# A spectral mixer and token MLP on one core: forward FFT over the sequence first, filter loaded in two copies, norm and first product streamed row block by row block

## The chip, the cores and the metric

One NeuronCore of a Trainium2 chip, one launch. The metric is the device time of one execution in microseconds (us). Each comparison ran both kernels on the same chip. A ratio is the mean time of one kernel's runs over the mean of the other's runs in the same rounds, so it is not quite the ratio of the medians quoted beside it. "Span" is the time from the first to the last instruction of the profiled execution; the time of a run is about 1.8 to 2.1 us longer.

Engines: PE is TensorE, DVE is VectorE, ACT is ScalarE, POOL is GpSimd, SP is SyncE, which only issues DMAs here.

## The reference, cut to what matters

```python
x = A_x                                    # [1, 2048, 512] bf16
h  = x + irfft2(rfft2(layernorm(x)) * (A_w_r + 1j * A_w_i))     # over sequence and features
u  = layernorm(layernorm(h))               # both over the 512 features
u  = gelu(einsum("bsd,sf->bdf", u, B_w1) + B_b1)                # 2048 -> 1376 over the sequence
y  = einsum("bdf,fs->bds", u, B_w2) + B_b2                      # 1376 -> 2048
return h + y.transpose(0, 2, 1)
```

## The kernel before

The sequence of 2048 lies in SBUF as 128 partitions by 16 row blocks. The program does not write instructions directly: it declares operations with the tiles they read and write, derives dependencies from the tiles' addresses, lets a list scheduler fix the order on each engine, and turns the remaining dependencies into semaphore waits. Both kernels do this, with two different builders.

```python
def sb_cells(self, ap):                      # which 32-byte cells does this access touch?
    h, lo, hi = self.tensors_by_hname[name]
    offs = np.array([int(ap.offset)], dtype=np.int64)
    dims = list(ap.ap)[1:]                   # the free dimensions; the partition dimension is left out
    for step, n in dims:
        offs = (offs[:, None] + step * np.arange(n)[None, :]).reshape(-1)
    byte_offs = lo + offs * esz
    ...
# op(): a read depends on the cell's last writer; a write on its last writer and all its readers
```

The head of its computation:

```python
for g in range(4):                                           # X in four loads of 512 KB
    dma(f"ld_x{g}", X[:, 4*g:4*g+4, :], x_psd[:, 4*g:4*g+4, :], ...)
dma("ld_wr", Wn[:, 0, :, :], A_w_r.rearrange("(k2 k1) k -> k1 k2 k", k1=NP), ...)   # filter, once
dma("ld_wi", Wn[:, 1, :, :], A_w_i.rearrange("(k2 k1) k -> k1 k2 k", k1=NP), ...)
lw1 = ln_stats(1, lambda s2: X[:, s2, :], NS2, gsz=4, prio=9)                    # DVE
# ... 64 PE transposes of X, then feature DFT: 64 matmuls of 512 columns,
#     rstd applied at the PSUM eviction
# ... 64 transposes of the filter, sequence FFT in two steps with 64 transposes between,
#     24 DVE operations for the complex filter product, inverse FFT,
# ... last inverse product: per row block 4 matmuls of 512 columns + 1 identity matmul adding X
# ... the two norms of h over all 16 blocks, then:
for t in range(NFT):            # first MLP product: 11 tiles x 16 blocks, then GELU in five operations
    for s2 in range(NS2): eng.matmul(ps[0:Mt, bank, :], lhsT, HH[:, s2, :], ...)
for s2 in range(NS2):           # second MLP product: 16 blocks x 11 tiles, bias and residual, store
    ...
```

## Time and profile before

Median 169.18 us of 4 runs (169.15 to 169.22). Span of the profiled run 167.1 us.

| Stretch of the chain | ends at, us |
|---|---|
| X, statistics, transposes, feature DFT | 27.9 |
| filter transposes | 31.4 |
| forward sequence FFT | 45.1 |
| filter product (VectorE) | 59.7 |
| inverse FFT | 67.7 |
| last inverse product | 79.6 |
| norms | 90.4 |
| first MLP product | 125.2 |
| GELU of the last tile | 128.4 |
| second MLP product | 163.7 |
| last block and store | 167.1 |

From the chain of work that ended last, in order of time. Columns: start, duration, engine, tile, line.

```profile
1.13 4.98 DMA X<-in_A_x_dram
6.13 2.48 DVE st_87 L657 x4
...
19.92 7.94 PE ps L738 x36
27.86 3.57 PE ps L719 x64
31.43 7.00 PE ps L769 x64
...
90.42 34.72 PE ps L1009 x160
...
128.35 35.26 PE ps L1033 x162
```

PE's issue intervals can be read here: 34.72 / 160 is 217 ns for 512 columns, 7.00 / 64 is 109 ns for 256, 3.57 / 64 is 56 ns for 128.

### The profile page before, as it was taken

What the parts mean: (1) busy time and instruction counts of PE and PEld (TensorE: products, weight loads), DVE (VectorE), ACT (ScalarE), POOL (GpSimd) and SP (SyncE); (2) the same over time, 40 slices, a digit from 0 to 9 for tenths busy, and PEclk for the clock granted to TensorE, in tenths of its full rate; (3) what the DMA queues carried; (4) which work ended last, traced back from release to release, by engine and by line L of the source; (5) the groups of instructions that cost most, each with busy time, mean ns of one, the idle gap of its engine ahead of it and who ended that gap; (6) DMA issues with size and microseconds to landing.
All of it is one profiled execution on the core that took longest, in us unless ns stands there. A gap on an engine that the chain in (4) does not pass through costs nothing.

```text
span 167.1 us, 2513 instructions
## 1 busy us (share of the span) xinstructions
PE 150.8 (90%) x912; PEld 90.8 (54%) x912; DVE 103.6 (62%) x251; ACT 75.8 (45%) x130; POOL 10.9 (6%) x23
## 2 busy tenths in 40 slices
PE   0599899998998689999995999999999999999991
PEld 0593346987546568544431444444455666666660
DVE  0599981987999979779998454354445322332231
ACT  3075897662599668456885644433432000000000
POOL 0000022200001070200060000000000000000000
PEclk9999999999999999999999999999999999999999
DMA  4999914283006659996039300000000111011101
GB/s 98 372 355 299 404 46 127 45 322 141 4 2 229 277 184 411 389 367 219 4 99 399 129 2 0 0 4 0 0 0 0 63 67 63 33 61 63 63 33 61
DMA packets 10123, 22.71 MB, mean 136 GB/s; under 512 B 928, under 2 KB 7328, under 8 KB 9472
## 3 DMA queue, kind: packets, MB, share of 16 engines
q0 software_dynamic: 2384, 13.90, 22.5%
q1 hardware_dynamic: 7728, 8.66, 15.9%
q8 instruction: 7, 0.11, 0.3%
q14 instruction: 4, 0.03, 0.1%
HBM read 20.46 MB, written 2.10 MB: 135 GB/s over the span
## 4 chain that ended last, share of the span: by engine, by line
PE 67%; DVE 24%; DMA 3%; ACT 3%; issue 1%; SPq 0%; ACTq 0%; DVEq 0%
PE ps L1033 21%; PE ps L1009 21%; DVE st_87 L657 6%; PE ps L918 6%; PE ps L738 5%; PE ps L769 4%; PE ps L892 4%; DMA X<-in_A_x_dram 3%; PE ps L797 2%; DVE st_89 L952 2%; PE ps L719 2%; DVE V_64 L846 1%; DVE V_64 L845 1%; PE ps L910 1%; PE ps L864 1%
## 5 line engine op out<-in xcount | busy, mean ns | idle before, releaser
L1038 DVE SCALAR_TENSOR_TENSOR OUT<-ps,B2f,H 128x512 bf16<-128x512 f32 x16 | 12.0, 751 | 24.2 <-PE ps L1033 24.2
L1009 PE MATMUL ps<-HH,W_b 128*128 128x512 bf16 (+1 forms) x66 | 16.6, 379 | 1.7 <-DVE HH L984 1.5
L918 PE MATMUL ps<-GD,V_51 128*128 128x512 bf16 x64 | 16.4, 379 | 0.0
L1009 PE MATMUL ps<-HH,W_a 128*128 128x512 bf16 (+1 forms) x66 | 16.1, 379 | 0.0
L738 PE MATMUL ps<-Esb,XT 128*128 128x512 bf16 x64 | 14.6, 380 | 1.0 <-DVE D_56 L747 0.6
L657 DVE BATCH_NORM_STATS2 st_87<-X 128x6 f32<-128x512 bf16 x16 | 9.9, 680 | 6.1 <-DMA X<-in_A_x_dram 6.1
L1009 PEld LDWEIGHTS ps<-HH,W_b 128*128 128x128 bf16 (+1 forms) x66 | 6.4, 100 | 10.0 <-DVE HH L984 2.2
L696 PE MATMUL ps<-ID,X 128*128 128x128 bf16 x64 | 6.1, 287 | 6.2 <-DMA X<-in_A_x_dram 6.2
L952 DVE BATCH_NORM_STATS2 st_89<-H 128x6 f32<-128x512 bf16 x16 | 10.8, 686 | 1.3 <-ACT H L926 1.0
L1009 PE MATMUL ps<-HH,W_c 128*128 128x512 bf16 (+1 forms) x44 | 11.3, 379 | 0.0
L738 PEld LDWEIGHTS ps<-Esb,XT 128*128 128x128 bf16 x64 | 5.8, 98 | 9.4 <-ACT XT L703 2.1
L1009 PEld LDWEIGHTS ps<-HH,W_a 128*128 128x128 bf16 (+1 forms) x66 | 6.5, 100 | 7.7 <-ACT HH L983 0.4
L926 ACT ACTIVATE H<-ps 128x512 bf16<-128x512 f32 x13 | 7.7, 595 | 6.4 <-PE ps L918 6.4
L864 PE MATMUL ps<-Hm,V_64 128*128 128x256 bf16 x64 | 8.2, 273 | 2.8 <-ACT TT L877 1.2
L918 PEld LDWEIGHTS ps<-GD,V_51 128*128 128x128 bf16 x64 | 6.2, 98 | 7.5
L830 ACT ACTIVATE Csb<-ps 128x512 bf16<-128x512 f32 x16 | 7.9, 680 | 4.3 <-PE ps L823 4.3
L877 ACT ACTIVATE TT<-ps 128x512 bf16<-128x512 f32 x16 | 8.5, 655 | 2.9 <-PE ps L864 2.8
L696 PEld LDWEIGHTS ps<-ID,X 128*128 128x128 bf16 x64 | 6.0, 134 | 6.2 <-issue 6.2
L864 PEld LDWEIGHTS ps<-Hm,V_64 128*128 128x128 bf16 x64 | 6.0, 98 | 5.0 <-ACT TT L877 2.1
L746 ACT ACTIVATE D_56<-ps,lnw_88 128x512 bf16<-128x512 f32 x13 | 8.1, 694 | 0.6 <-PE ps L738 0.4
L900 DVE CAST V_51<-ps 128x256 bf16<-128x256 f32 x19 | 7.2, 420 | 1.3 <-PE ps L892 1.2
L703 ACT ACTIVATE XT<-ps 128x1024 bf16<-128x1024 bf16 x8 | 7.6, 1017 | 0.0
(118 smaller groups left out, 274.5 us busy)
## 6 DMA issues: line engine op xcount, KB each, us to landing
W_a<-in_B_w_dram POOLq DMA_DIRECT2D x1, 2064.0 KB, 7.6
W_b<-in_B_w_dram POOLq DMA_DIRECT2D x1, 2064.0 KB, 10.4
X<-in_A_x_dram SPq DMA_DIRECT2D x4, 512.0 KB, 6.2
IFP<-c_IFP POOLq DMA_DIRECT2D x1, 2048.0 KB, 9.1
out_dram<-OUT SPq DMA_DIRECT2D x16, 128.0 KB, 1.7
FP<-c_FP SPq DMA_DIRECT2D x1, 1536.0 KB, 10.9
W_c<-in_B_w_dram POOLq DMA_DIRECT2D x1, 1376.0 KB, 6.1
Wn<-in_A_w_r_dram SPq DMA_DIRECT2D x1, 1028.0 KB, 11.0
```

What stands on the lines that cost most here:

```text
L657: o = K.op(f"ln{which}_stats{s2}", "dve", (lambda s, eng, bank, src=src, s2=s2: eng.bn_stats(st[:, s2, 0:6], src)), ins=[src], outs=[st[:, ...
L696: (lambda s, eng, bank, lhsT=lhsT, i=i: eng.matmul(psb[:, bank, i * 128:(i + 1) * 128], lhsT, ID[:, :], is_transpose=True, start=True, sto ...
L738: (lambda s, eng, bank, lhsT=lhsT, rhs=rhs, t=t: eng.matmul(ps[:, bank, :], lhsT, rhs, start=(t == 0), stop=(t == 3))),
L746: return eng.activation(dst, src, ACT.Copy, scale=sc)
L830: return eng.activation(dst, src, ACT.Copy)
L864: eng.matmul(ps[:, bank + ci // 2, (ci % 2) * 256:(ci % 2) * 256 + 256], lhsT, rhs, start=(comp == 0), stop=(comp == 1))),
L877: return eng.activation(dst, src, ACT.Copy)
L918: (lambda s, eng, bank, lhsT=lhsT, rhs=rhs, mi=mi: eng.matmul(ps[:, bank, :], lhsT, rhs, start=False, stop=(mi == 3))),
L952: K.op(f"ln2_stats{s2}", "dve", (lambda s, eng, bank, src=src, s2=s2: eng.bn_stats(st2[:, s2, 0:6], src)), ins=[src], outs=[st2[:, s2, 0:6 ...
L1009: (lambda s, eng, bank, lhsT=lhsT, rhs=rhs, s2=s2, Mt=Mt: eng.matmul(ps[0:Mt, bank, :], lhsT, rhs, start=(s2 == 0), stop=(s2 == NS2 - 1))),
L1033: (lambda s, eng, bank, lhsT=lhsT, rhs=rhs, t=t: eng.matmul(ps[:, bank, :], lhsT, rhs, start=(t == 0), stop=(t == NFT - 1))),
L1038: (lambda s, eng, bank, dst=dst, bia=bia, hs=hs: eng.scalar_tensor_tensor(dst, ps[:, bank, :], bia, hs, op0=ALU.add, op1=ALU.add)),
```

## The change

The intent is to stream fewer columns through PE and to close its holes. The sequence FFT comes first, taken on X itself, so X needs no transposes. The mean is never subtracted: the filter's column for feature frequency 0 is dropped by both kernels. The row scale 1/std is multiplied into the 128 x 128 DFT block of each row block instead of into the data. Real and imaginary parts of a frequency sit on neighbouring partitions, so the filter product is one DVE operation per chunk, and this needs the filter in SBUF twice, once for the real and once for the imaginary row. The inverse is done block by block, and its result goes through residual, norm and six of the eleven tiles of the first MLP product at once. GELU is one ScalarE activation.

The new builder's tracker, the new filter load and the new head, cut to the core (`+` lines of the diff):

```diff
+    def cells_of(self, ap):
+        lo = self.tensors[ap.tensor.name]
+        ...
+        offs = np.array([int(ap.offset)], dtype=np.int64)
+        for step, n in list(ap.ap)[1:]:
+            if n > 1:
+                offs = (offs[:, None] + step * np.arange(n, dtype=np.int64)[None, :]).reshape(-1)
+        b = lo + offs * esz
...
+    pieces = [(0, 8), (8, 18), (18, 32)]
+    for pi, (ta, tb) in enumerate(pieces):
+        for comp, wsrc in enumerate((A_w_r, A_w_i)):
+            q = "sp" if comp == 0 else "pool"
+            for reim in range(2):
+                for j in range(2):
+                    for sgn in range(2):
+                        p0 = 4 * j + 2 * sgn + reim
+                        ...
+                            dma(f"ld_w{comp}_{pi}_{p0}_{a}", q, W[p0:NP:8, a:b, comp, :], src, ...,
+                                prio=1.0 + pi, group=f"W{pi}{q}", wgroup=f"W{pi}")
+    K.op("mk_eps", "dve", lambda e, eng: eng.memset(eps[:, 0:1], LN_EPS), outs=[eps[:, 0:1]], ...)
...
+    for g in range(8):
+        # bn_stats, bn_aggr on DVE; sqrt on ACT ("sd"); reciprocal on DVE ("rs"); then for both blocks
+                K.op(f"fs{n2}_{s}", ("pool" if g < 7 else "dve"),          # scale the DFT block
+                     lambda e, eng, ...: eng.tensor_scalar(FS[:, n2, ...], F[:, n2, :], rs[:, n2, 0:1], ...))
+        # first product: 4 matmuls of 256 columns per block
+        K.op(f"Ye{g}", "act", emit_y, ins=[ps[:, b0:b0 + 2, :]], outs=[dst], ...)
```

## The prediction

> **What bounds the kernel now.** The page gives PE 90% of a 167.1 us span (wall time 169.18, so 2.1 us lie outside it). The chain of waits, in order of time: X lands at 6.1; norm statistics, X transposes and the first product until 27.9; filter transposes to 31.4; forward FFT to 45; the filter multiply, bound by VectorE (24 operations of 0.60 us), to 59.7; inverse FFT to 67.7; last inverse product (64 matmuls plus 16 identity matmuls of 512 columns) to 79.6; a second norm with almost no PE work until 90.4; first MLP product 34.7 us; a GELU chain of 3.2 us; second product 35.3 us; 2.7 us of tail. Full-rate issue intervals from the same chain: 217 ns at 512 columns, 109 at 256, 56 at 128.
>
> **Removed.** 128 PE transposes, the 16 identity matmuls and half of several products: 344,064 streamed columns become 278,528. With those intervals PE work falls from about 147 to 119 us (MLP products unchanged at 38 us each). Also 16 of the 24 filter multiplies' worth of VectorE time, the PE hole of the second norm (about 5 us of idle), and four operations of each GELU.
>
> **Added or moved.** The filter is loaded twice over, as 52 small DMAs of 512-byte runs, half issued from GpSimd. GpSimd also scales 28 of the 32 DFT blocks, and stands *behind* its 26 DMA issues. The DMA issues back to back there take 0.53 us each in the trace, so about 15 us pass before the first scaled block. The Trainium skill, "DMA: Bandwidth & Descriptors", SWDGE vs HWDGE vs iDMA, says a GpSimd core computes these descriptors in software; the 0.53 us agrees. A scale of 128x128 has no counterpart in the trace; from "GPSIMD Engine Reference", section 3.1 (about 1.8 cycles per element plus dispatch), I estimate 0.35 us. So the first product is GpSimd-bound: 15 + 28 x 0.35, all of Y at about 28 us, though X is ready by 10.
>
> **Middle** (16 chunks: column DFT, 16-point DFT, filter, inverse 16-point). PE 8 x 109 + 8 x 56 = 1.32 us a chunk; ScalarE about 1.17 (evictions back to back 0.50); VectorE about 1.03. With stalls 1.4, plus a fill of 3.5: ends near 54.
>
> **Streamed part.** A hole of 2 to 3 us while the first rows go through eviction, product, add, square, root, apply. Then PE per row block is 4 x 109 + 217 + 2 x 109 + 6 x 217 = 2.17 us, against ScalarE about 1.55 and VectorE about 1.25: PE-bound. Remaining PE work 49.5 us plus 2 us of stalls: first product done near 110. GELU wait 1 us, second product 38 us, tail 2.7: span 152.
>
> **Prediction: 154 us, range 144 to 162.** Faster by over 2%: 0.93; within 2%: 0.05; slower: 0.02.
>
> **What would show the steps.** GpSimd busy with DMA issues until about 15 us, then scaling until about 25, with PE waiting for it; column DFTs starting near 28; middle about 26 us with PE about 90% busy; no PE idle beyond 3 us at the start of the streamed part; row blocks at 2.2 to 2.3 us; mm2 unchanged at 38 us.
>
> **What would make it wrong.** GpSimd issues or scales much faster than I take (down to about 145) or stalled by descriptor backlog (up to 162); filter pieces landing late; the static order of instructions stalling the middle chunks at 1.7 us rather than 1.4 (5 us more); ScalarE's in-order queue delaying the streamed rows.

## More of the kernel before

From the page of the kernel before. The first lines are busy time, share of the span and instruction count of each engine; the second part cuts the span into 40 slices, one digit for the busy tenths of each.

```profile
span 167.1 us, 2513 instructions
PE 150.8 (90%) x912; PEld 90.8 (54%) x912; DVE 103.6 (62%) x251; ACT 75.8 (45%) x130; POOL 10.9 (6%) x23
...
PE   0599899998998689999995999999999999999991
...
DVE  0599981987999979779998454354445322332231
```

PE starts in the second slice and hardly pauses. DVE starts there too, when the first piece of X lands.

No load of the kernel before starts at any partition but 0.

## The result, and the profile after

Median 175.56 us of 4 runs (174.75 to 177.18), against 169.18; ratio 1.0391, 95% interval 1.0335 to 1.0446. The kernel is slower than the one before, and 21.6 us above the prediction's 154.

From the page of the changed kernel:

```profile
span 174.4 us, 2045 instructions
PE 125.1 (72%) x775; PEld 78.9 (45%) x784; DVE 62.4 (36%) x142; ACT 63.2 (36%) x130; POOL 26.7 (15%) x64
...
PE   0000000088858999685989889899999999999992
...
DVE  0000000788507786836453455510000333223331
...
POOL 7994000069630100000000000000000000000000
```

PE's work did fall, from 150.8 to 125.1 us busy. But PE does nothing in the first eight slices, and neither does DVE in the first seven. One slice is 4.4 us.

From the chain of the changed kernel:

```profile
0.74 2.70 DMA X<-in_A_x_dram
3.44 28.04 issue
31.48 0.08 DVE st L509
...
34.69 0.73 POOL FS L521 x2
...
39.75 4.94 PE ps L535 x24
...
49.78 0.62 PE ps L572 x4
...
75.88 1.48 PE ps L680 x12
...
133.18 2.32 PE ps L757 x10
...
171.24 0.75 DVE OUT L763
```

X's first piece landed at 3.44. Then the chain has 28.04 us called "issue", which means only that the profile shows nothing the engine waited for. Set against the forecast:

| Stretch | forecast, us | measured, us |
|---|---|---|
| head, until the column DFTs start | 28 | 49.8 |
| middle (column DFTs, filter, inverse) | 26 | 26.1 |
| streamed part and rest of the first MLP product | 56 | 57.3 |
| GELU wait | 1 | under 0.1 |
| second MLP product | 38 | 38.1 |
| tail | 2.7 | 3.2 |

The measured rows are differences of the chain's start times above; the GELU wait is the 0.05 us before the line at 133.18. The miss of 22 us is the head, and all of it. SyncE's queue of the changed kernel in order of time (start, duration, queue, line, operation, tiles, count):

```profile
7.82 21.22 SPq L459 DMA_DIRECT2D W<-in_A_w_r_dram  x26
```

GpSimd in order of time; in brackets, the idle time before the line and what ended it:

```profile
1.27 13.98 POOL L459 DMA_DIRECT2D W<-in_A_w_i_dram  x26 [0.82 <-POOLq L825]
34.69 2.82 POOL L521 TENSOR_SCALAR FS<-F,rs 128x128 bf16<-128x128 bf16 x8 [19.43 <-DVE mv L511]
```

GpSimd was through with its DMA issues at 15.25, as forecast, and then waited another 19.43 us for DVE. SyncE issued its last filter load at 29.0. DVE began 2.4 us later. The page gives 3.1 us in the median from the start of an issue to the landing for the largest of these loads, so the last one landed just before.

Why would statistics of X wait for the filter? The compiled program's wait list tells it (it is no view of the profile). The first instructions of DVE:

```
1 L499 Memset eps 128x1 [waits sem_dg5]
2 L509 BNStats st<-X 128x6 [waits sem_d0]
3 L500 Memset eps 128x1 [waits sem_dve]
4 L511 BNStatsAggregate mv<-st 128x2 [waits sem_dve,sem_dg3]
```

`dg5` is the semaphore of the third piece of the real filter, on SyncE; `dg3` of the third piece of the imaginary filter, on GpSimd. A memset of one constant waits for the last filter load. It does not need it. The tracker takes the offset of an access, which for a tile in SBUF counts the partition in units of one partition's row, and adds it as if it were a place within the row. The filter tile W has 32 x 2 x 256 = 16,384 elements, 32,768 bytes in each partition, at byte 61,952. A load that starts at partition 3 therefore seems to begin at 61,952 + 3 x 32,768 = 160,256. The third piece holds places 18 to 31 of W's first dimension of 32, 1,024 bytes each, so it seems to reach from 178,688 to 193,024. The statistics lie there: `st` at 186,880, `mv` at 187,392, `eps` at 191,168 (sums over the tile sizes in the kernel's `memory_layout`). The tracker sees a write after a write and orders them. The loads of a piece share one semaphore, so DVE waits for all eight.

This is theory A. Theory B, the rival, was that the load traffic itself holds the head: 52 small loads share the DMA engines with X and the DFT blocks. Its premise has something in it: the last piece of X landed at 18.95 us in the changed kernel (the longest of X's loads took 12.9 us from issue to landing), against 9.89 in the kernel before. The question is whether that holds the head.

### The profile page after: what moved, and what is told of

The parts are those of the page before. It is cut to its first block, busy times and chain, and to the rows that moved or that the text cites. A ratio compares the mean times of both kernels' runs of the same rounds, so it can differ in the third digit from the quotient of the medians.

```text
span 174.4 us, 2045 instructions
## 1 busy us (share of the span) xinstructions
PE 125.1 (72%) x775; PEld 78.9 (45%) x784; DVE 62.4 (36%) x142; ACT 63.2 (36%) x130; POOL 26.7 (15%) x64
## 4 chain that ended last, share of the span: by engine, by line
PE 62%; issue 18%; ACT 8%; DVE 8%; DMA 2%; POOL 1%; DVEq 0%
PE ps L751 20%; PE ps L714 19%; PE ps L535 5%; PE ps L623 4%; PE ps L589 4%; PE ps L680 3%; DVE H L695 2%; ACT Y L546 2%; PE ps L689 2%; PE ps L572 2%; ACT SQ L698 2%; DMA X<-in_A_x_dram 2%; ACT Xsb L598 1%; PE ps L757 1%; DVE HH L706 1%
## 5 line engine op out<-in xcount | busy, mean ns | idle before, releaser
L714 PE MATMUL ps<-HH,W 128*128 128x512 bf16 (+1 forms) x171 | 40.8, 379 | 4.1 <-DVE A L704 2.1
L535 PE MATMUL ps<-FS,X 128*128 128x256 bf16 x64 | 11.5, 357 | 36.7 <-POOL FS L521 36.3
L751 PE MATMUL ps<-GT,W 128*128 128x512 bf16 (+1 forms) x162 | 35.7, 379 | 0.2
L751 PEld LDWEIGHTS ps<-GT,W 128*128 128x128 bf16 (+1 forms) x165 | 23.8, 144 | 11.9
L714 PEld LDWEIGHTS ps<-HH,W 128*128 128x128 bf16 (+1 forms) x176 | 17.0, 100 | 20.9 <-issue 4.0
L509 DVE BATCH_NORM_STATS2 st<-X 128x6 f32<-128x512 bf16 x16 | 10.2, 669 | 31.5 <-issue 31.5
L698 ACT ACTIVATE SQ<-H,nm 128x512 bf16<-128x512 bf16 x16 | 11.5, 717 | 9.4 <-DVE H L695 9.4
L459 POOL DMA_DIRECT2D W<-in_A_w_i_dram x26 | 14.0, 551 | 0.8 <-POOLq L825 0.8
L695 DVE TENSOR_TENSOR H<-ps,X 128x512 bf16<-128x512 f32 x16 | 10.9, 689 | 7.7 <-PE ps L692 7.7
L605 DVE TENSOR_TENSOR P<-Xsb,W 128x1024 bf16<-128x1024 bf16 x16 | 10.6, 685 | 5.5 <-ACT Xsb L598 5.4
```

What stands on the lines that cost most here:

```text
L459: return eng.dma_start(dst, src)
L535: r = eng.matmul(ps[:, b, 256 * u:256 * u + 256].rearrange("p (a b) -> p a b", a=2), X[:, n2, 128 * t:128 * t + 128], fr if t < 2 else fa, ...
L695: K.op(f"h{n2}", "dve", lambda e, eng: eng.tensor_tensor(H[:, n2, :], ps[:, bA, :], X[:, n2, :], ALU.add), ins=[ps[:, bA, :], X[:, n2, :]] ...
L698: K.op(f"sq{n2}", "act", lambda e, eng: eng.activation(sq[:, :], H[:, n2, :], ACT.Square, bias=nm[:, n2, 0:1], accum_out=s2t[:, n2, 0:1]), ...
L714: return eng.matmul(ps[0:Mt, bank, :], W1[:, n2, 128 * t:128 * t + Mt], HH[:, n2, :], start=(n2 == 0), stop=(n2 == 15), skip_group_check=True)
L751: r = eng.matmul(ps[:, b, :], W2[t][0:Kt, n2::16], GT[0:Kt, t, :], start=(t == 0), stop=(t == NFT - 1), skip_group_check=True)
```

## The experiments

All outputs are right. Executions over 1.5% slower than the fastest of the same kernel are left out of the means. "Changed" is the changed kernel.

### e1a: the same order, true waits only

The scheduler plans as before, with the false dependencies, so every instruction keeps its place on every engine. The waits are then derived from addresses without the partition part. All false waits go, not only the one on DVE's first instruction.

```diff
-        offs = np.array([int(ap.offset)], dtype=np.int64)
+        off0 = int(ap.offset)
+        if row:                                   # row: for the waits, not for the plan
+            off0 %= int(np.prod(ap.tensor.shape[1:]))
+        offs = np.array([off0], dtype=np.int64)
...
     K.schedule()
+    for o in K.ops:
+        o.deps = o.true_deps
     K.gen_sync()
```

> The changed kernel with every instruction in the same place on every engine; only the semaphore waits are derived again, from addresses without the partition part. Theory A (VectorE's first instruction waits for the last piece of the filter because the program's own address tracker takes a load that starts at partition 1 to 7 for a write into other tiles): VectorE starts at 3 to 4 us instead of 31.5; GpSimd then binds as forecast, first scale at 15.3, last at about 25.5; column DFTs start near 28 instead of 49.8; time 152 to 156. Theory B (the head is held by the load traffic itself, X and the DFT blocks arriving late behind 52 small filter DMAs): VectorE still starts late, time 168 or more.

Measured: 156.55 us median (156.37 to 158.21); before 169.17; ratio 0.9276 (0.9228 to 0.9323). DVE of this run in order of time:

```profile
0.81 0.06 DVE L537 MEMSET eps<- 128x1 f32 x1 [0.81 <-PEq L867]
3.41 0.69 DVE L547 BATCH_NORM_STATS2 st<-X 128x6 f32<-128x512 bf16 x1 [2.54 <-DMA X<-in_A_x_dram]
```

And POOL:

```profile
1.26 13.93 POOL L497 DMA_DIRECT2D W<-in_A_w_i_dram  x26 [0.82 <-POOLq L867]
15.31 2.80 POOL L559 TENSOR_SCALAR FS<-F,rs 128x128 bf16<-128x128 bf16 x8
19.59 1.41 POOL L559 TENSOR_SCALAR FS<-F,rs 128x128 bf16<-128x128 bf16 x4 [1.48 <-DVE mv L549]
```

And from its chain:

```profile
20.36 5.14 PE ps L573 x24
25.52 1.02 ACT Y L584
26.55 0.20 ACT sd L552
...
30.60 0.62 PE ps L610 x4
```

The memset ran at 0.81 us instead of 31.5, the first statistics when X came. The scales started at 15.31, right behind the DMA issues. The column DFTs started at 30.6 instead of 49.8. The head gained 19.2 us, and the median 175.56 - 156.55 = 19.0 us. Theory B is refuted as the cause of these 19 us: the same loads, in the same order, are still there. X still lands late, at 19.43 for the last piece, but DVE's last wait for X ended at 12.3.

The median is 0.55 us above the range of theory A, and the head is 2.6 us longer than forecast. GpSimd stood still for 1.9 us in three short waits for DVE (the 1.48 above is the longest). But from 20.3 on the chain is not on GpSimd at all: it follows the first product, 24 matmuls in 5.14 us, which is 214 ns each and not the 109 of the forecast, then an eviction ("Y"), and a square root ("sd") that stands behind the eviction on ScalarE. So GpSimd binds only the first part of this head. The profiled run is the one of 158.21, with a mean granted clock of 0.989; the other three, 156.37 to 156.68, had 0.997 to 1.0. The profile records a granted clock of one half in it from 32.0 to 35.4, after the head.

### e3: the last filter piece later

The changed kernel with its false waits, and eight more loads on SyncE ahead of the last piece.

```diff
+    for i in range(8):                            # a tile nobody reads
+        K.op(f"again{i}", "sp", lambda e, eng, i=i: eng.dma_start(T["AGAIN"][i:NP:8, :, :], again[:, 16+i:36+i:2, 1:257]),
+             occ=450.0, prio=2.5, nbytes=16 * 512 * 10)
```

> The changed kernel with its waits as they are, and eight more filter loads of 80 KB (into a tile that nobody reads, without waits) on the SyncE queue ahead of the last eight. The 26 filter issues of that queue took 21.2 us, 0.82 each, so the last piece should land about 6.5 us later. Theory A: VectorE's first instruction moves by the same 6.5 us, from 31.5 to about 38, and the time by the same, to about 182. Theory B, or any cause other than the wait for that piece: VectorE's start does not move with it by the same amount; X, which was loaded before, is not delayed, and the time stays within 2 us of 175.6.

Measured: 180.98 us median; runs 180.42, 180.98 and 180.98, and one of 184.01; ratio 1.0681 (1.0659 to 1.0703). SP's queue in this run, in order of time:

```profile
23.98 5.12 SPq L479 DMA_DIRECT2D AGAIN<-in_A_w_r_dram  x8
29.14 5.15 SPq L460 DMA_DIRECT2D W<-in_A_w_r_dram  x8
```

And DVE in order of time:

```profile
36.80 0.69 DVE L514 BATCH_NORM_STATS2 st<-X 128x6 f32<-128x512 bf16 x1 [36.80 <-issue]
```

The eight loads took 5.12 us to issue, not 6.5: the average of 0.82 us over 26 issues was too high for these. DVE's start moved by 36.8 - 31.5 = 5.3 us and the median by 180.98 - 175.56 = 5.4 us. The cost follows the last filter piece one for one. Theory A says so, and we could think of no other cause that does.

### e1: the tracker put right

The one line for plan and waits alike.

```diff
-        offs = np.array([int(ap.offset)], dtype=np.int64)
+        offs = np.array([int(ap.offset) % int(np.prod(ap.tensor.shape[1:]))], dtype=np.int64)
```

> One line of the address tracker corrected, so that the list scheduler plans without the false waits as well; it then puts four scales on GpSimd after 12 of its 26 DMA issues, not all after the 26th. GpSimd's total work in the head is the same (26 issues of 0.54 and 28 scales of 0.35, about 24 us from 1.3), so theory A expects the last scale at the same 25 to 26 us and the time within 2 us of the run that keeps the order, 151 to 156. Theory B: 168 or more.

Measured: 158.01 us median (157.45 to 158.30); ratio 0.9336 (0.9316 to 0.9356). This is 2 us above the range for the run itself, and within 2 us of e1a as expected. GpSimd's last scale ended at 26.8; the column DFTs started at 30.2, as in e1a. All runs of e1 had a mean granted clock of 0.987 to 0.989, like the one slow-clocked run of e1a, which took 158.21. So the plan without false dependencies gains nothing by itself, as far as that one run can tell. That GpSimd's total work sets the end is not shown. The chain leaves GpSimd after two scales, and goes on with

```profile
20.58 6.67 PE ps L535 x36
```

which is 185 ns each (213 at first, 109 from 25.7 on). GpSimd by itself would have let the product go faster: two scales of 0.35 us are 0.70 us for the four matmuls of a block, and four matmuls at 213 ns are 0.85. Here too the first product at its low rate binds.

The expectations below call this the low clock. What the traces show of it: the matmuls of 256 columns start 213 ns apart early in the first product (eight in 1.89 us, from 10.18 in this run) and 109 ns apart later. In e4 the profile records a granted clock of 0.5 from 26.2 to 36.5, and there too eight of them took 1.89 us (from 29.80); in e6's second run eight took 1.05 (from 20.81). For the early stretch the views print a granted clock of 1.00, but the traces hold no clock record before 25.2 in e1a and 25.9 in e1, about where the interval falls to 109 ns, and a stretch without a record is counted as 1.00.

### e4: the scales on VectorE

```diff
-                K.op(f"fs{n2}_{s}", ("pool" if g < 7 else "dve"),
+                K.op(f"fs{n2}_{s}", "dve",
```

(On top of e1.)

> As the corrected tracker, and all 32 scales on VectorE instead of 28 on GpSimd. If GpSimd is what binds the head once the false wait is gone, VectorE (16 statistics of 0.60, aggregates and reciprocals, 32 scales of about 0.13, from 3.5) should be done at about 20 to 21 us, column DFTs start at 22 to 24 instead of about 28, and the time falls by another 4 to 6 us, to 147 to 151. If X's arrival (last piece at 12.9) or the products at the low clock bind instead, it falls by under 2 us.

Measured: 160.01 us median (159.26 to 161.49); ratio 0.9469 (0.9416 to 0.9523). The expectation failed: the gain of 4 to 6 us is not there. The column DFTs start at 32.8, against 30.2 in e1. The chain shows why:

```profile
17.91 1.02 ACT Y L546
18.94 0.19 ACT sd L514
...
19.16 0.17 DVE rs L516
...
19.40 0.39 DVE FS L521 x2
...
19.83 3.37 PE ps L535 x16
...
23.22 1.02 ACT Y L546
...
32.80 1.89 PE ps L572 x8
```

This is a loop of 5.3 us for two groups, 17.91 to 23.22. ACT takes its instructions in the order of the program. The square root ("sd") that the next scale needs stands behind an eviction ("Y"), although the last statistics before it were done at 16.9. The eviction waits for the first product, which runs at 3.37 / 16 = 211 ns a matmul here, twice the 109 ns seen before. That product in turn waits for the scale. The same link of eviction and root stood in e1a's chain. How much longer the head became through the edit alone is not known: all four runs of e4 had a mean granted clock of 0.956 to 0.968, against 0.987 to 0.989 for e1, and the stretch at 0.5 from 26.2 to 36.5 covers the last 14 matmuls of the first product. At 104 ns more for each, that is about 1.5 of the 2.6 us (an estimate from the 213 and 109 ns above). Whether the edit itself brought the lower clock is not shown.

### e6: roots ahead of evictions

On top of e4, the eviction of group g must come after the root of group g + 2.

```diff
+    for g in range(8):                            # products and evictions now in a loop of their own
...
-        K.op(f"Ye{g}", "act", emit_y, ..., prio=2 + g)
+        K.op(f"Ye{g}", "act", emit_y, ..., prio=2 + g,
+             after=[o for o in K.ops if o.name == f"sd{min(g + 2, 7)}"])
```

> As the run with all scales on VectorE, but ScalarE must take the square root of group g+2 before it evicts group g of the first product. Theory: in that run ScalarE's in-order queue closed a loop (eviction, root, reciprocal, scale, two groups of product at the low clock, eviction: 5.3 us for two groups, four times round), which ate the gain. Then VectorE and X's arrival (about 13 us) bind: the last eviction of the first product ends at 26 to 27 instead of 32.7, and the time falls by about 6 us, to 152 to 155. Rival: the first product itself binds, 64 matmuls at 213 ns at the low clock; then the time stays within 2 us of 160.

Measured: 153.47, 153.58 and 155.47 us; ratio 0.9117 (0.9057 to 0.9176). The profiled run took 273.26 us and is left out as a slow one; it is told in the last section. The median, 153.58, is 6.4 us below that of e4, as the loop theory said, but on another chip and mostly at a higher granted clock. At a like clock the gain is 4 to 5 us: 155.47 at 0.967, against 159.63 and 160.40 at 0.968 in e4. Because the profile was of no use, the same kernel was run again:

> The run with roots ahead and all scales on VectorE once more, beside the one that splits the scales, because its profiled execution fell in a slow state with half-rate matmuls throughout (271.5 us). Expected 153 to 155.5 in fast runs; in its profile the last eviction of the first product ends at 26 to 28, against 32.7 before the roots were moved, and the 5.3 us loop through ScalarE is gone.

Measured: 152.77 us median (152.04 to 153.45), just under the range expected; ratio 0.9031 (0.8998 to 0.9064). The chain of this run:

```profile
20.45 0.63 DVE FS L521 x4
21.08 0.60 DVE st L509
21.85 0.74 DVE FS L521 x4
...
26.69 0.62 PE ps L574 x4
```

The loop is gone, and statistics and scales alternate on DVE. The column DFTs start at 26.7 instead of 32.8. The rival, that the first product at its low rate binds by itself, is refuted.

### e7: X ahead of the filter on the DMA engines

On top of e6, GpSimd's filter loads wait for the last piece of X.

```diff
+    x_in = [o for o in K.ops if o.name == "ld_x14"]
-                                prio=1.0 + pi, group=...
+                                prio=1.0 + pi, after=x_in if q == "pool" else (), group=...
```

> As the run before, and GpSimd's 26 filter loads wait until the last piece of X has landed, so that X and the DFT blocks do not share the DMA engines with them. If X's arrival binds the head (it came at 13 to 14 us with the filter loads beside it), X is there at 9 to 10, the last eviction of the first product ends at 22 to 24 and the time falls by another 2 to 4 us, to 149 to 152. The filter must still come in time: its last GpSimd piece at about 30, needed at about 38. If X's arrival does not bind, the time changes by under 1 us; if the filter comes late, it rises.

Measured: 152.91, 153.60 and 154.54 us; ratio 0.9087 (0.9044 to 0.9131), which e6's interval overlaps. No gain is shown. The edit did less than was meant: the last piece of X landed at 14.9 us, against 18.9 in e6's second run, and not at 9 to 10; and the third piece, the last that DVE waited for, came no earlier, at 8.8 against 8.1. So the arrival of the later pieces does not bind, and that of the third, which starts DVE's long stretch, was not tested. In this profile (a run of 155.78 us, counted as slow) DVE worked from 8.8 to 25.4 with hardly a gap, so the time per row block on DVE was underrated: (25.4 - 8.8) / 14 blocks is 1.2 us, against the 1.05 or so that e4's expectation implies (done at 20 to 21 from 3.5, for 16 blocks).

### e8: the scales split between VectorE and GpSimd

On top of e6.

```diff
-                K.op(f"fs{n2}_{s}", "dve",
+                K.op(f"fs{n2}_{s}", ("dve" if g < 4 else "pool"),
```

> As the run with roots ahead and all scales on VectorE, but only groups 0 to 3 are scaled on VectorE and groups 4 to 7 on GpSimd, after its 26 DMA issues (from 15.3). In the run with X first VectorE was busy without a gap from 8.8 to 25.4, so VectorE seems to bind the head now; taking 16 scales of 0.17 off it should end its statistics near 21 and the last eviction of the first product near 25, against 27.9, and give 150 to 152 against 153.5. If the first product at the low clock binds, or X, the time stays within 1 us of 153.5.

Measured: 152.08 us median of 6 runs (151.76 to 153.94); ratio 0.8989 (0.8974 to 0.9004). The chain of this run:

```profile
20.17 3.17 POOL FS L521 x9
23.38 0.62 PE ps L536 x4
24.03 1.03 ACT Y L547
25.11 0.62 PE ps L574 x4
```

The median is 0.08 us above the range expected. The column DFTs start at 25.1, as expected, 1.6 us before e6's second run on the same chip. The median is only 0.7 us lower, and the two intervals overlap a little, so a gain of e8 over e6 is likely but not shown. e8's ratio of 0.8989 to the kernel before, the lowest of all, is 10% off the time.

## Why the prediction was wrong

- **"So the first product is GpSimd-bound: 15 + 28 x 0.35, all of Y at about 28 us, though X is ready by 10."** This is the step that failed, and with it the 154 us. It took the statistics to start when X lands, and so saw only one wait in the head, that for GpSimd. In the changed kernel DVE started at 31.5, because a false dependency made its first instruction wait for the last filter load. e1a takes the false waits away, moves no instruction, and gets 156.55 us; e3 delays the awaited load by 5.1 us and pays 5.4 us.
- **Two smaller parts of the same step were off as well.** X was not ready by 10: its last piece landed at 18.95, and at 19.43 in e1a. And with the false waits gone GpSimd bound only the first part of the head; from 20.3 on it was the first product at 214 ns a matmul, where the forecast had 109, and then the root behind the eviction. The column DFTs started at 30.6 instead of 28. What each of these is worth was not tested. That e1a still comes within 2.6 us of the 154 is in part luck: the product at its low rate, 0.85 us a block, happens to be little slower than GpSimd at 0.70.
- **The costs on GpSimd were right.** Its 26 issues took 14.0 us (forecast: 0.53 each, about 15 from the start). Its scales took 0.353 us each back to back, 2.82 / 8 with the first one's start-up, against the estimate of 0.35 worked out from the Trainium skill, "GPSIMD Engine Reference", section 3.1. That GpSimd computes the descriptors in software, as the prediction takes from "DMA: Bandwidth & Descriptors", SWDGE vs HWDGE vs iDMA, is shown by no run here; SyncE's 26 issues took longer, 0.82 us each.
- **Middle, streamed part, second product** were right to 0.1, 1.3 and 0.1 us. PE's busy time fell by 25.7 us, against 28 forecast.
- **"What would make it wrong"** listed faster or stalled issues and scales on GpSimd, filter pieces landing late, stalls by the static order and ScalarE's order in the streamed rows. It did not list a wait that the data do not call for. The evidence was at hand before the run: the wait list of the compiled program has `sem_dg5` at the first DVE instruction.

So the change gives 10% once other things are put right with it. The tracker is worth 19 us (e1a). Scaling on VectorE with the roots ahead of the evictions brings a further 4 us or so (158.01 in e1 to 153.58 in e6; the chips differ, but at a like clock, 0.987 to 0.989, the runs are 157.45 to 158.30 and 153.47). The split of the scales may add a little. Roots ahead with the scales left on GpSimd was not tried, though e1a's chain passes through the same link.

What stays open: why the mean granted clock differs between runs of one kernel (0.989 to 1.0 in e1a, worth about 1.7 us there) and between kernels (0.956 to 0.968 in e4).

## What to carry to other kernels

When dependencies are derived from addresses, a new kind of access (here a load that starts at a partition other than 0) can hit a corner that the old kernel never touched; read the semaphore waits of the first few instructions on every engine, and ask of each whether the data call for it. "Issue" in front of DVE's first instruction was no cost of issuing here: it was a wait that the profile did not name. And when an in-order engine serves both ends of a loop, moving work to a faster engine may lengthen it, so look at what stands in front of the short instruction that the loop needs.

## What the Trainium skill lacked or had wrong

- "DMA: Bandwidth & Descriptors", section Issuing engines are not separate DMA queues, says that the time saved by issuing from several engines is usually small relative to the DMA. For one load that held here: 0.54 us of GpSimd's time, against 6.3 to 6.8 us from issue to landing for the larger ones. For many small loads in a row the sum counts: 26 loads of 8 to 112 KB cost GpSimd 13.98 us, in which the trace shows no other work on it.
- "TensorE: Matmul & The Clock Gate", Part 1, says that the array's clock is released after about 3.4 us of sustained activity. One run of e6 ran at about half the usual rate from end to end: 273.26 us, with PE busy 252.0 of a span of 271.5 us, and 60 matmuls of 512 columns in 28.26 us, 471 ns each, where 217 is usual. The same part warns that clock records of a trace have been unreliable and that the gate has been seen stuck at a quarter for 50 us and more; it has no case of half the rate for a whole run. The granted clock of 1.000 that the result lists says nothing: this trace holds no clock record, and its page has no PEclk row. The cause is open. The first lines of its page:

```profile
span 271.5 us, 2046 instructions
PE 252.0 (93%) x775; PEld 118.2 (44%) x784; DVE 68.4 (25%) x170; ACT 67.0 (25%) x130; POOL 16.8 (6%) x36
```

  And one line of its PE in order of time:

```profile
157.95 28.26 PE L716 MATMUL ps<-HH,W 128*128 128x512 bf16 x60 [0.28 <-issue]
```

- "Perfetto Trace Analysis", section Identifying Dependency Chains, says to look at an instruction's text for the semaphores it waits on. That was right here and is what found the cause: 31.5 us stood under "issue" in the profile, and the wait list named the filter loads.
- "GPSIMD Engine Reference", section 3.1, agrees in sum: the estimate from it was 0.35 us for a scale of 128 x 128, the trace has 0.353. But its cycles give only 128 x 1.8 / 1.2 GHz = 0.19 us of that (an estimate from the page). For the dispatch that makes up the rest it gives a time for VectorE and none for GpSimd.
